# Moving the decay products of a fused SSD + FFN kernel into its prologue, with five halves ahead of pair 1's D

## The chip, the cores and the metric

One core of a Trainium2 chip. The metric is the time of one execution on the device, in microseconds (us). A profile is of one further execution; its span leaves out about 1.7 us of start and end. PE is the matmul engine (PEld its weight loads), DVE is VectorE, ACT ScalarE, POOL GpSimd, SP the queue that issues most loads.

A single execution counts as "slow" here when it lies over 1.5% above the fastest of the same kernel.

## The reference

A chunked state-space layer (4 batches, 8 heads, 768 tokens, head size 32, state size 16), then a gated FFN on its output (3072 tokens, 256 to 1536 to 256). Cut to what matters:

```python
log_a = np.log(np.clip(a, 1e-6, 1.0))          # a in [0.85, 0.95]
for c in range(nc):                            # chunks of 32 tokens
    cum = np.cumsum(la, axis=-1)
    y_intra = (C B^T * exp(cum_i - cum_j) * causal) @ x
    y_inter = (C @ state) * exp(cum)
    state = exp(sum(la)) * state + sum_j B_j x_j * exp(cum_last - cum_j)
out = (np.maximum(y @ w_gate, 0) * (y @ w_val)) @ w_out
```

The kernel works on pairs of 128 tokens. The decay factors are running products of `a`, put into token order by small fp32 products with a picking matrix.

## The kernel before

All engines keep the order of the program. The prologue scales B and C of pair 0, turns them (transposes on PE), forms G = B C^T, masks it, and gets y = (masked G) x + (state) C. That is evicted to `yT`, and the FFN starts: `gvh(b, f, u)` is one "half", four matmuls of 256 columns for feature block f and half-block u of 256 tokens. In the code `adds` is the product of B and x for the state, `inter_wide` that of C and the state, `D_wide` ("D" below) that of the masked G and x, and `decays` ("dec") a small product for the decay of whole chunks. Dummies keep PE busy.

```python
NSHARED = 5                       # five PSUM banks shared; three more: "tp" (turn), "y", "Aps"

def keep_warm(n, rhs=warm):       # warm is a 128x128 bf16 tile of zeros
    w = bank("w", (128, 128))
    for _ in range(n):
        nc.tensor.matmul(out=w, lhsT=warm, rhs=rhs, start=True, stop=True)

def decay():                      # bank "tp"; all batches; fp32
    ...
    for r in range(2):
        for i in range(2):        # 4 products, 64 columns of weights, 8 of output
            nc.tensor.matmul(out=d3[64*i:64*i+64, r], lhsT=cp[:, i*128+r:i*128+128:2],
                             rhs=pick[:, 0, NH:2*NH], ...)
    for k in range(HC):           # 3 products, 128 columns of weights, 64 of output
        nc.tensor.matmul(out=d[:, k]..., lhsT=cp[:, k*128:(k+1)*128], rhs=pick..., ...)

# the order of the program, cut
keep_warm(22); d = factors(); decays(0); keep_warm(8)
...                               # weights' guard and issues, C and B of pair 0 scaled
transp(0, 1, False); keep_warm(4); transp(0, 0, True); tevac(0, A_, V)
scan(0, H); scale_wide(1, 1, P_); scale_wide(1, 0, P_); keep_warm(6)
G_wide(0); keep_warm(7); ...; decays(1); adds(0); ...
inter_wide(0); D_wide(0, ...); turn(1, True); keep_warm(2); yevac_wide(0, A_, V)
load_bc(2, 1, nc.sync); load_bc(2, 0, nc.sync)
...
f0 = gvh(0, 0, 0, True); G_wide(1); decay(); adds(1)
...                               # masks of pair 1, f0()
late = [gvh(0, f, 0, True) for f in (1, 2, 3)]
inter_wide(1); D_wide(1); late[0](); late[1](); yevac_wide(1, A_, V)
late += [gvh(0, f, 0, True) for f in (4, 5)]
for fin in late[2:]: fin()
decay_factors(); ...; halves(0, 1, 0, 1, 2, 3, 4, 5); gv(0, 6)   # u=1, then full blocks
```

## Time and profile before

| | before |
|---|---|
| time, median of 4 fast executions | 124.38 us (124.36 to 124.89) |
| span of the profile | 122.7 us |
| PE busy, share of the span | 118.1 us, 96% |
| first half f0 on PE | 10.53 us |
| G of pair 1 on PE | 11.09 us |
| first half of u=1 on PE | 15.76 us |

Because PE does not wait from 12.77 us to the end, the last row is the one to compare. The prediction shows the lines. Four more of PE, from the timeline of the kernel before (start, length, engine, line, operation; the start-to-start distance of neighbours is the real cost, since the ends are modelled):

```profile
5.79 0.50 PE L189 MATMUL w<-warm 128*128 128x128 bf16 x6
...
10.53 0.38 PE L686 MATMUL gv<-yT,wg 128*128 128x256 bf16 x2
...
11.09 0.42 PE L418 MATMUL g<-CT,BT 32*64 32x256 bf16 x16
...
15.76 0.38 PE L686 MATMUL gv<-yT,wg 128*128 128x256 bf16 x2
```

### The profile page before, as it was taken

The page shows a single profiled execution, that of the slowest core. Times are in us where ns is not written, and L with a number is a line of the kernel's source. Part 1 is how long each engine was busy: PE and PEld are TensorE (multiplying, and loading weights), DVE is VectorE, ACT ScalarE, POOL GpSimd, SP SyncE. Part 2 cuts the span into 40 slices and gives each one's busy share as a digit, 9 for nine tenths or more (in the row PEclk, how much of TensorE's full clock was granted, in tenths as well). Part 3 has the DMA queues.
Part 4 walks back from the last instruction along what each step waited for, and adds up shares of the span by engine and source line. Part 5 has one row for each costly group of instructions (what it writes and reads, how often), then busy time and mean ns, then how long its engine had stood idle before and what let it go on. Part 6 is the DMA issues. An engine that isn't in the chain of part 4 may idle for free.

```text
span 122.7 us, 3665 instructions
## 1 busy us (share of the span) xinstructions
PE 118.1 (96%) x1404; PEld 82.4 (67%) x1404; DVE 88.0 (72%) x200; ACT 76.3 (62%) x169; POOL 48.2 (39%) x108
## 2 busy tenths in 40 slices
PE   6989999999999999999999999999999999999990
PEld 6856784577875478874577864677854678844790
DVE  4798988872799864988763897855987656788410
ACT  0467688835987725786635886545877447876420
POOL 6499989361455127360351806033600033000000
DMA  3999999996979995999999498960580002200022
GB/s 63 220 208 146 171 192 194 189 172 103 115 89 139 143 142 143 103 150 205 150 114 140 154 136 138 110 117 0 189 52 0 0 0 91 85 0 0 0 91 86
DMA packets 77489, 13.93 MB, mean 113 GB/s; under 512 B 70064, under 2 KB 77472, under 8 KB 77472
## 3 DMA queue, kind: packets, MB, share of 16 engines
q1 hardware_dynamic: 70128, 10.61, 54.2%
q0 software_dynamic: 4288, 2.36, 14.1%
q10 hardware_dynamic: 3056, 0.72, 2.7%
q8 instruction: 11, 0.18, 0.6%
q14 instruction: 6, 0.05, 0.1%
HBM read 11.13 MB, written 3.15 MB: 116 GB/s over the span
## 4 chain that ended last, share of the span: by engine, by line
PE 92%; POOL 4%; DVE 1%; issue 1%; DVEq 0%
PE o L713 26%; PE gv L686 21%; PE gate L668 15%; PE val L671 15%; PE y L643 2%; PE g L548 2%; PE w L189 2%; POOL wg L199 2%; POOL bs L322 1%; PE y L632 1%; PE o L707 1%; PE A_ps L601 1%; PE g L418 1%; POOL wv L199 1%; PE y L523 1%; PE dec L262 1%
## 5 line engine op out<-in xcount | busy, mean ns | idle before, releaser
L675 DVE TENSOR_TENSOR h<-r,val 128x512 bf16<-128x512 bf16 x44 | 30.0, 685 | 7.3 <-ACT r L674 7.2
L713 PE MATMUL o<-wo,h 128*128 128x256 bf16 x276 | 33.1, 273 | 0.0
L674 ACT ACTIVATE r<-gate 128x512 bf16<-128x512 f32 x44 | 26.3, 597 | 9.7 <-PE gate L668 9.3
L713 PEld LDWEIGHTS <-h 128*128 128x128 bf16 x276 | 25.9, 98 | 5.3 <-issue 1.7
L668 PE MATMUL gate<-yT,wg 128*128 128x512 bf16 x88 | 26.2, 379 | 0.0
L671 PE MATMUL val<-yT,wv 128*128 128x512 bf16 x88 | 26.2, 379 | 0.0
L692 DVE TENSOR_TENSOR h<-r,gv 128x256 bf16<-128x256 bf16 x56 | 22.5, 419 | 2.6 <-ACT r L689 1.8
L689 ACT ACTIVATE r<-gv 128x256 bf16<-128x256 f32 x56 | 21.2, 386 | 2.3 <-PE gv L686 0.2
L686 PE MATMUL gv<-yT,wg 128*128 128x256 bf16 x112 | 21.5, 273 | 0.0
L686 PE MATMUL gv<-yT,wv 128*128 128x256 bf16 x112 | 21.4, 273 | 0.0
L556 POOL TENSOR_SCALAR_AFFINE_SELECT gs<-gs 128x512 bf16<-128x512 bf16 (+1 forms) x16 | 8.0, 523 | 30.0 <-ACT gs L567 30.0
L573 DVE TENSOR_TENSOR gs<-g,maskUT 128x512 bf16<-128x512 f32 x16 | 10.3, 685 | 11.4 <-issue 5.6
L338 POOL TENSOR_TENSOR tok<-bcr,scaleBC 128x128 bf16<-128x128 f32 x32 | 12.2, 409 | 14.1 <-DMA bcr<-in_B_dram 13.0
L671 PEld LDWEIGHTS <-wv 128*128 128x128 bf16 x88 | 8.6, 98 | 10.4
L668 PEld LDWEIGHTS <-wg 128*128 128x128 bf16 x88 | 8.6, 98 | 8.9
L686 PEld LDWEIGHTS <-wv 128*128 128x128 bf16 x112 | 11.0, 98 | 1.3
L686 PEld LDWEIGHTS <-wg 128*128 128x128 bf16 x112 | 10.2, 98 | 1.9 <-DVE yT L536 0.2
L567 ACT CAST gs<-g 128x512 bf16<-128x512 f32 x8 | 4.7, 589 | 6.7 <-PE g L548 6.7
L656 ACT CAST yT<-y 128x512 bf16<-128x512 f32 x8 | 4.7, 586 | 5.1 <-PE y L643 2.5
L433 DVE TENSOR_TENSOR gs<-g,wmask 128x512 bf16<-128x512 f32 x9 | 5.9, 680 | 2.6 <-PE g L418 2.6
L189 PE MATMUL w<-warm 128*128 128x128 bf16 x49 | 5.5, 284 | 1.1 <-DVE tmask L163 1.1
L189 PEld LDWEIGHTS <-warm 128*128 128x128 bf16 x58 | 5.0, 126 | 1.7 <-DVE tmask L163 1.1
(122 smaller groups left out, 115.8 us busy)
## 6 DMA issues: line engine op xcount, KB each, us to landing
xr<-in_x_dram SPq DMA_DIRECT2D x17, 128.0 KB, 3.2
out_dram<-ob SPq DMA_DIRECT2D x3, 512.0 KB, 3.2
bcr<-in_C_dram SPq DMA_DIRECT2D x17, 64.0 KB, 2.9
bcr<-in_B_dram SPq DMA_DIRECT2D x17, 64.0 KB, 2.9
out_dram<-ob SPq DMA_DIRECT2D x4, 256.0 KB, 3.5
xr<-in_x_dram SPq DMA_DIRECT2D x3, 256.0 KB, 4.1
wo<-in_moe_w_out_dram POOLq DMA_DIRECT2D x2, 384.0 KB, 8.5
wg<-in_moe_w_gate_dram POOLq DMA_DIRECT2D x4, 128.0 KB, 4.0
```

Source lines behind the costliest of these rows:

```text
L189: nc.tensor.matmul(out=w, lhsT=warm, rhs=rhs, start=True, stop=True)
L338: eng.tensor_tensor(out=dst[:, t, j * (1 + t)], in0=src[:, j, :, t], in1=f[:, j, :, 4 * t:4 * t + 4].to_broadcast([128, 2, 4, N]), op=ALU. ...
L556: nc.gpsimd.affine_select(out=dst, in_=dst, pattern=[[0, n], [1, 128]], compare_op=ALU.is_ge, fill=0.0, base=0, channel_multiplier=-1)
L573: nc.vector.tensor_tensor(out=d[:, q], in0=g[q], in1=m, op=ALU.mult)
L668: nc.tensor.matmul(out=g, lhsT=wg[:, k, fs], rhs=yT[:, k, tk], start=(k == 0), stop=(k == 1))
L671: nc.tensor.matmul(out=v, lhsT=wv[:, k, fs], rhs=yT[:, k, tk], start=(k == 0), stop=(k == 1))
L674: nc.scalar.activation(r, g, AF.Relu)
L675: nc.vector.tensor_tensor(out=fst[b][:, f], in0=r, in1=v, op=ALU.mult)
L686: nc.tensor.matmul(out=gv_[:, j], lhsT=w[:, k, fs], rhs=yT[:, k, tk], start=(k == 0), stop=(k == 1), skip_group_check=True)
L689: nc.scalar.activation(r, gv_[:, 0], AF.Relu)
L692: nc.vector.tensor_tensor(out=fst[b][:, f, u * 256:(u + 1) * 256], in0=r, in1=gv_[:, 1], op=ALU.mult)
L713: nc.tensor.matmul(out=o[:, ts % 2], lhsT=fst[b][:, f, ts * 128:(ts + 1) * 128], rhs=wo[:, f], start=(f == 0), stop=(f == NF - 1), skip_gr ...
```

## The change

Its intent: take 1.15 us of fp32 decay products out of the stretch where PE does useful work and put them among the dummies; use the turn bank, free by then, for half f1, so that four halves instead of three stand ahead of pair 1's D; let DVE scale pair 1's B. Its core, with cuts:

```diff
-    a_sb = glob.tile([2 * BH, H], FP32)                 # all batches
+    RL = 2 * (NB - 1) * NH                              # batches 1 to 3: 48 rows for 64
+    nc.scalar.dma_start(out=a_sb, in_=a[1:]...)
...
 def decay(w):
-        # 4 products of 64 weight columns
+        # 2 products of 128 weight columns
         for k in range(HC):
             nc.tensor.matmul(...)
+            if k < HC - 1:
+                nc.tensor.matmul(out=w, lhsT=warm, rhs=warm, start=True, stop=True)
...
-    decays(0)
-    keep_warm(8)
+    nc.vector.memset(wg[0:1, 0, 0:1], 0.0)              # the weights' guard, earlier
+    for f in (0, 2, 4):
+        weights(f, f + 2)
+    decays(0)
+    keep_warm(6)
...
     keep_warm(4)
+    decays(1)                                           # was behind G(0)
     transp(0, 0, True)
...
-    keep_warm(6)
+    keep_warm(4)
     G_wide(0)
     keep_warm(7)
+    adds(0)
     gcopy(0, 0)
     gmask(0, 2, V, True)
-    keep_warm(5, st[0]["gw"][:, 0, 0, 0])               # and 4 more below
+    middle()
+    decay(keep_warm(2))
...
+    tevac(1, None, A_)
+    copy_B(1, V)
     weights(6, 8)
     weights(8, NF)
     weights_out(0, NF // 2)
     weights_out(NF // 2, NF)
     cast_x(1, V)
+    load_bc(2, 1, nc.sync)                              # was ahead of the weights
+    load_bc(2, 0, nc.sync)
...
-    late = [gvh(0, f, 0, True) for f in (1, 2, 3)]
+    late = [gvh(0, 1, 0, True, mm.tile([128, 2, 256], FP32, tag="tp", name="gv1"))]
+    late += [gvh(0, f, 0, True) for f in (2, 3, 4)]
+    late[0]()
     inter_wide(1)
     D_wide(1)
+    late[1]()
+    yevac_wide(1, A_, V)
     late[0]()                                           # these three lines stay:
     late[1]()                                           # work done twice
     yevac_wide(1, A_, V)
```

More of the change, by code (lines that the diff above doesn't have):

```diff
@@ L138 @@
     load_bc(0, 0, nc.sync, nc.scalar)
-    a_sb = glob.tile([2 * BH, H], FP32)
-    nc.sync.dma_start(out=a_sb, in_=a.rearrange("b h (w s) -> (b h w) s", w=2))
+    RL = 2 * (NB - 1) * NH
+    a_sb = glob.tile([RL, H], FP32)
+    nc.scalar.dma_start(out=a_sb, in_=a[1:].rearrange("b h (w s) -> (b h w) s", w=2))
     load_x(0, nc.sync, nc.scalar)
@@ L176 @@
     cp0 = glob.tile([R, 128], FP32)
-    pick = const.tile([2 * BH, 2, BH], FP32)
-    pairs = identf.rearrange("p (h w) -> p w h", w=2)
+    pick = const.tile([RL, 2, RL // 2], FP32)
+    pairs = identf[0:RL, 0:RL].rearrange("p (h w) -> p w h", w=2)
     nc.vector.tensor_copy(pick[:, 1], pairs[:, 1])
@@ L189, in keep_warm @@
             nc.tensor.matmul(out=w, lhsT=warm, rhs=rhs, start=True, stop=True)
+        return w
     wg = glob.tile([128, 2, DF], BF16)
@@ L232, in decays, with scan, decay @@
         nc.scalar.copy(out=dec, in_=d)
-    cp = glob.tile([2 * BH, H], FP32)
-    rmid = const.tile([2 * BH, 1], FP32)
-    def scan(s0, s1):
+    cp = glob.tile([RL, H], FP32)
+    rmid = const.tile([RL, 1], FP32)
+    def scan():
         nc.vector.tensor_tensor_scan(
-            out=cp[:, s0:s1], data0=a_sb[:, s0:s1],
-            data1=zero1.to_broadcast([2 * BH, s1 - s0]),
-            initial=cp[:, s0 - 1:s0] if s0 else 1.0, op0=ALU.mult, op1=ALU.add)
+            out=cp, data0=a_sb, data1=zero1[0:RL].to_broadcast([RL, H]),
+            initial=1.0, op0=ALU.mult, op1=ALU.add)
+        nc.vector.reciprocal(rmid, cp[:, H - 1:H])
     def middle():
-        nc.vector.reciprocal(rmid, cp[:, H - 1:H])
-        nc.vector.tensor_scalar_mul(pick[:, 0], pairs[:, 0], rmid)
+        nc.scalar.mul(pick[:, 0], pairs[:, 0], rmid)
     fac3 = glob.tile([128, 2, 2, NH], FP32)
     scaleBC = glob.tile([128, NB, NC, 2, 8], FP32)
-    def decay():
-        bank_ = mm.tile([128, HC * 2 * NB * 8 + 16], FP32, tag="tp", name="dec")
-        n = HC * 2 * NB * 8
-        d = bank_[:, 0:n].rearrange("p (k w b h) -> p k w b h", k=HC, w=2, b=NB)
-        st["dec3"] = d3 = bank_[:, n:n + 16].rearrange("p (r h) -> p r h", r=2)
-        for r in range(2):
-            for i in range(2):
-                nc.tensor.matmul(
-                    out=d3[64 * i:64 * i + 64, r], lhsT=cp[:, i * 128 + r:i * 128 + 128:2],
-                    rhs=pick[:, 0, NH:2 * NH], start=(r == 0), stop=True,
-                    tile_position=(0, 64 * i), skip_group_check=True)
+    def decay(w):
+        n = HC * 2 * (NB - 1) * NH
+        bank_ = mm.tile([128, n + 2 * NH], FP32, tag="tp", name="dec")
+        d = bank_[:, 0:n].rearrange("p (k w b h) -> p k w b h", k=HC, w=2, b=NB - 1)
+        st["dec3"] = d3 = bank_[:, n:].rearrange("p (r h) -> p r h", r=2)
+        turned = cp[:, 0:256].rearrange("p (i m r) -> p r i m", i=2, r=2)
+        for r in range(2):
+            nc.tensor.matmul(
+                out=d3[:, r], lhsT=turned[:, r], rhs=pick[:, 0, 0:NH], start=(r == 0),
+                stop=True, skip_group_check=True)
         for k in range(HC):
@@ L274, in decay_factors @@
             nc.scalar.copy(
-                out=scaleBC[:, :, cs, 1, :].rearrange("p b k h -> p k b h"), in_=d[:, :, w])
+                out=scaleBC[:, 1:, cs, 1, :].rearrange("p b k h -> p k b h"), in_=d[:, :, w])
     def inverse(b0, b1):
@@ L319, in scale_wide @@
         src = s["bcr"].rearrange("s (t q) j r n -> s j r t q n", t=2)[:, j]
-        f = wfac[:, j, :, :, p]
+        f = fac[:, :, :, 0] if p == 0 and j else wfac[:, j, :, :, p]
         for t in range(2):
@@ L371, in tevac @@
         s = st[p]
-        tp = s.pop("tp")
+        tp = s["tp"]
+        if beng is None:
+            s["CT"] = CT = att.tile([128, 2, 2, 128], BF16, tag="CT", name="CT")
+            for t in range(2):
+                nc.scalar.mul(
+                    CT.rearrange("s t i m -> s t (i m)")[:, t].rearrange(
+                        "s (m r) -> s m r", r=2),
+                    tp[1].rearrange("s r m -> s m r"), tmask[:, t:t + 1])
+            return
         s["BT"] = BT = att.tile([128, 2, 128], BF16, tag="BT", name="BT")
@@ L477, in carry @@
             nc.vector.scalar_tensor_tensor(
-                out=n, in0=T_.pop(c - 1), scalar=dec[:, c - 1:c], in1=st[p]["A"][i],
+                out=n, in0=T_[c - 1], scalar=dec[:, c - 1:c], in1=st[p]["A"][i],
                 op0=ALU.mult, op1=ALU.add)
@@ L675, in gv, with gvh @@
         nc.vector.tensor_tensor(out=fst[b][:, f], in0=r, in1=v, op=ALU.mult)
-    def gvh(b, f, u, later=False):
+    def gvh(b, f, u, later=False, where=None):
         if f == 0 and u == 0:
@@ L682, in gvh @@
         fs = slice(f * 128, (f + 1) * 128)
-        gv_ = bank("gv", (128, 2, 256))
+        gv_ = where or bank("gv", (128, 2, 256))
         for j, w in ((0, wg), (1, wv)):
@@ L768 @@
     keep_warm(22)
-    d = factors()
+    fac = factors()
+    nc.vector.memset(wg[0:1, 0, 0:1], 0.0)
+    for f in (0, 2, 4):
+        weights(f, f + 2)
     decays(0)
-    keep_warm(8)
-    nc.vector.tensor_copy(wfac[:, 1], d)
-    nc.vector.memset(wg[0:1, 0, 0:1], 0.0)
-    weights(0, 2)
-    weights(2, 4)
-    weights(4, 6, (0,))
+    keep_warm(6)
     scale_wide(0, 1, V)
-    nc.vector.reciprocal(wfac[:, 0, :, :, 0], wfac[:, 1, :, :, 0])
+    nc.vector.reciprocal(wfac[:, 0, :, :, 0:2], fac[:, :, :, 0:2])
+    nc.scalar.copy(out=wfac[:, 1], in_=fac)
     scale_wide(0, 0, V)
@@ L781 @@
     keep_warm(4)
+    decays(1)
     transp(0, 0, True)
     tevac(0, A_, V)
-    nc.vector.reciprocal(wfac[:, 0, :, :, 1:3], wfac[:, 1, :, :, 1:3])
-    scan(0, H)
+    scan()
+    cast_x(0, A_)
     scale_wide(1, 1, P_)
-    scale_wide(1, 0, P_)
-    weights(4, 6, (1,))
-    keep_warm(6)
+    keep_warm(4)
     G_wide(0)
     keep_warm(7)
+    adds(0)
     gcopy(0, 0)
     gmask(0, 2, V, True)
-    keep_warm(5, st[0]["gw"][:, 0, 0, 0])
-    cast_x(0, A_)
-    decays(1)
-    adds(0)
+    middle()
+    decay(keep_warm(2))
+    gcopy(0, 1)
+    gmask(0, 0, V)
+    gmask(0, 1, V)
     gmask(0, 3, V, True)
-    keep_warm(4, st[0]["gw"][:, 3, 0, 0])
-    gmask(0, 0, V)
-    gmask(0, 1, V, True)
     pass_on(0, 0)
     carry(0, 0)
-    middle()
+    decay_factors()
+    scale_wide(1, 0, V)
     inter_wide(0)
-    D_wide(0, (2, 3, 0))
-    D_wide(0, (1,))
+    D_wide(0, (2, 0, 1))
+    D_wide(0, (3,))
     turn(1, True)
@@ L810 @@
     yevac_wide(0, A_, V)
-    load_bc(2, 1, nc.sync)
-    load_bc(2, 0, nc.sync)
-    carry(0, 1)
+    tevac(1, None, A_)
+    copy_B(1, V)
     weights(6, 8)
@@ L817 @@
     weights_out(NF // 2, NF)
-    tevac(1, V, A_)
     cast_x(1, V)
-    pass_on(0, 1)
+    load_bc(2, 1, nc.sync)
+    load_bc(2, 0, nc.sync)
+    carry(0, 1)
+    f0 = gvh(0, 0, 0, True)
     def halves(b, u, *fs):
@@ L823, in halves @@
             gvh(b, f, u)
-    f0 = gvh(0, 0, 0, True)
     G_wide(1)
-    decay()
     adds(1)
     gcopy(1, 0)
-    gmask(1, 2, V, True)
-    f0()
-    gcopy(1, 1)
-    gmask(1, 3, V, True)
-    carry(1, 0)
+    gmask(1, 3, V, True)
+    gcopy(1, 1)
+    gmask(1, 0, V)
+    gcopy(1, 2)
+    carry(1, 0)
+    gmask(1, 1, V)
+    pass_on(0, 1)
+    f0()
     pass_on(1, 0)
-    gmask(1, 0, V)
-    gmask(1, 1, V)
-    late = [gvh(0, f, 0, True) for f in (1, 2, 3)]
+    gmask(1, 2, V)
+    late = [gvh(0, 1, 0, True, mm.tile([128, 2, 256], FP32, tag="tp", name="gv1"))]
+    late += [gvh(0, f, 0, True) for f in (2, 3, 4)]
+    late[0]()
+    nc.vector.reciprocal(wfac[:, 0, :, :, 2], wfac[:, 1, :, :, 2])
     inter_wide(1)
     D_wide(1)
+    late[1]()
+    yevac_wide(1, A_, V)
     late[0]()
@@ L843 @@
     yevac_wide(1, A_, V)
-    late += [gvh(0, f, 0, True) for f in (4, 5)]
     for fin in late[2:]:
         fin()
-    decay_factors()
+    halves(0, 0, 5, 6)
     scale_wide(2, 1, P_)
@@ L861 @@
                           wmask.rearrange("p k (m r) -> p k r m", r=2))
-    halves(0, 1, 0, 1, 2, 3, 4, 5)
-    gv(0, 6)
+    halves(0, 1, 0, 1, 2, 3, 4, 5, 6)
     carry(1, 1)
```

## The prediction

> **What bounds the kernel now.** I read the page's busy table first, then the chain of work that ended last, then the first 16 us of the timeline engine by engine, then stretches of busy time.
>
> ```profile
> PE 118.1 (96%) x1404; PEld 82.4 (67%) x1404; DVE 88.0 (72%) x200; ACT 76.3 (62%) x169; POOL 48.2 (39%) x108
> ...
> PE 92%; POOL 4%; DVE 1%; issue 1%; DVEq 0%
> ```
>
> PE (the matmul engine) is busy 96% of the 122.7 us span and is 92% of the chain. The waits view gives PE only 1.5 us of idle time, all before 11 us. After that it never waits, so the time is: when useful matmuls begin to run back to back, plus a fixed amount of work. A change of the first 16 us counts only by what it does to that date. The stretches (columns: length, then busy time of PE, PEld, DVE, ACT, POOL, then clock, DMA share, GB/s):
>
> ```profile
> 8.00:12.77 4.77, 4.50 (x118) 3.16 (x118) 4.26 (x13) 3.28 (x10) 4.75 (x9) 1.00 1.23 162
> 12.77:15.74 2.97, 2.97 (x84) 2.35 (x69) 2.75 (x8) 1.81 (x6) 2.97 (x5) 1.00 1.31 168
> ```
>
> From 12.77 PE is full, but DVE (VectorE) is 2.75 of 2.97 us busy too: it is nearly as tight here. In the chain (start, length), the decay product of all batches sits inside the useful stretch, between pair 1's G and the FFN halves:
>
> ```profile
> 11.13 0.39 PE g L418 x16
> 11.51 0.34 PE dec L257 x8
> 11.85 0.81 PE dec L262 x6
> 12.84 1.42 PE gv L686 x12
> ```
>
> That is 1.15 us of PE which the change wants to hide under the dummy matmuls at 8 us. The durations used below are these rows of DVE and ACT (start, length, line, operation):
>
> ```profile
> 10.19 0.84 ACT L385 ACTIVATE CT<-tp,tmask 128x256 bf16<-128x256 bf16 x2
> 11.55 1.07 ACT L437 CAST gs<-g 128x512 bf16<-128x512 f32 x2
> 11.62 0.69 DVE L433 TENSOR_TENSOR gs<-g,wmask 128x512 bf16<-128x512 f32 x1 [0.40 <-PE g L418]
> 13.16 0.27 DVE L477 SCALAR_TENSOR_TENSOR T<-T,dec,y 128x64 f32<-128x64 f32 x1
> 13.35 0.75 DVE L433 TENSOR_TENSOR gs<-gs,wmask 128x512 bf16<-128x512 bf16 x2
> 14.12 0.75 DVE L692 TENSOR_TENSOR h<-r,gv 128x256 bf16<-128x256 bf16 x2
> 15.07 0.42 DVE L540 CAST yT<-Aps 128x256 bf16<-128x256 f32 x1 [0.20 <-PE Aps L523]
> ```
>
> Consecutive instructions overlap by some 0.07 us, so I count starts to starts: mask from PSUM 0.62, mask from SBUF 0.37, carry 0.20, an h product 0.36, a yT eviction 0.36 on DVE; G copy 0.49, relu of a half 0.32 on ACT; a half (4 matmuls of 256 columns) 0.437 on PE.
>
> **What the Trainium skill says.** "Perfetto Trace Analysis", Identifying the Most-Contended Engine: matmul busy share is no good measure of distance from the roofline. Agreed: the 96% includes 58 dummies, so I go by the chain. "TensorE: Matmul & The Clock Gate", LDWEIGHTS: the load goes by columns, not by contraction rows. The trace agrees: the 48-row and the 64-row fp32 loads of 128 columns both cost 0.135 to 0.145 us a step, 64 columns only 0.04; so going from 64 to 48 rows saves nothing per instruction. Same page, What's actually happening: PE runs at half rate until it has been busy for some 3.4 us. Here 22 dummies take 0.115 us each, and those at 5.8 us take 0.08; fewer dummies might delay that, but PE stays filled. "VectorE: DVE Perf Modes", The perf-mode tier table: a tensor_tensor gains from bf16 in SBUF, not from PSUM. Agrees: 0.69 against 0.41 us.
>
> **Part by part.**
> (a) Front. The weights' guard memset moves ahead of pair 0's scaling, so POOL starts the weight issues at about 3.5 instead of 4.73 us and makes all six in a row. C of pair 0 is scaled straight from PSUM: the 0.21 us copy leaves DVE, but the reciprocal grows from 0.25 to 0.34. The dec product (2 instructions, 0.3 us) now stands before the turn of B on PE, so that turn starts at about 5.7 as before (5.67), and G(0) at 6.45 (was 6.42). On DVE the 0.34 us second reciprocal is gone, so the scan starts at 6.0 (was 6.39) and ends at 6.9.
> (b) Decay in the prologue. ACT does cast x (6.4 to 7.0), G copy (to 7.55), pick (to 7.75). Decay then starts at about 7.8: 2 fp32 matmuls for d3 and 3 for d are 10 instructions (each is two) x 0.135 = 1.35, plus two dummies 0.15: PE is taken until 9.3. Before, pair 0's inter product started at 8.97. So the decay is not wholly free: pair 0's inter and D run 9.3 to 9.87, against 9.83 before, only because D no longer waits for its masks (DVE: the last mask ends at about 9.3).
> (c) Pair 1's B on DVE: 0.49 us at 9.3 to 9.8, in the place where DVE did rmid and pick (0.5 us, moved to earlier and to ACT). B is ready at 9.8 instead of 10.23, but the turn of C now waits for the decay factors' copies to leave the turn bank: ACT 9.45 to 9.87, so 9.94 (was 9.84). yT(0) is done at 10.4 (was 10.38), CT, 0.84 us of ACT after it, at 11.06 (was 11.03). G(1) starts at 11.1 (was 11.09). The earlier B gains nothing, because CT sets G(1).
> (d) Pair 1. PE: G to 11.5, adds to 11.73, f1 at once in the turn bank (free since CT), f2, f3, f4 in G's banks as copy and masks free them (12.25 onwards), until 13.57. DVE: mask 3 at 11.63, mask 0, carry, mask 1, f0, mask 2: 0.62 + 0.37 + 0.20 + 0.37 + 0.36 + 0.37, ends 13.92. D runs 13.95 to 14.3; before it ended at 14.87 with one half fewer done. So up to D the change is ahead by 14.87 + 0.437 - 14.3 = **1.0 us**: roughly the 1.15 us of decay.
> (e) After D. The diff, read literally, runs the product of f2 and the yT eviction, and then the products of f1 and f2 **and the eviction once more**. Nothing removes them, and the first u=1 half reads yT after its last write. DVE after mask 2: f1 waits for its relu on ACT (three G copies, two states, then relu, ends 13.96), runs at 14.02; reciprocal 14.38; f2 14.55; yT 14.9; f1 again 15.25; f2 again 15.62; yT again 15.98 to 16.40. PE can start u=1 at 16.48 (was 15.74). It has f5 and f6 in front, 0.87 us, to 15.17, and then stands idle 1.3 us.
> Sum: 16.48 - 0.437 (one half more done) - 15.74 = **+0.30 us**. Without the repeats u=1 would start at about 15.4, and the same sum gives about -0.75.
> Afterwards DVE has f3 to f6 in hand, 1.5 us late, but a product (0.36 to 0.39) is shorter than a half (0.437) and five banks carry the lag; no further loss. Time: 124.37 + 0.30, and 0.1 for the DMA risk below: **124.75 us**.
>
> **Rivals.**
> 1. Repeats hidden, decay hidden: -0.75 to -1.0 us, 123.5 us. For it: PE is the bound, 1.15 us leave its path. Against: DVE's list from G(1) to u=1 is 4.7 us of work with no slack, and it sets u=1.
> 2. DMA becomes the wait in front. The engines' page shows 220 GB/s from 3 us on; weights starting 1.2 us sooner compete with x(0), which ACT now needs at 6.4 rather than 7.4. x issued at 2.3 to 2.4 with 3.3 us to landing comes at 5.7, but two more 128 KB weights in flight are 256 KB / 220 GB/s = 1.2 us of traffic in the worst case. A late cast moves the G copy, pick and decay: up to +0.5, 125.2 us. Against: the q0 queue's own start is slow (4 us to landing), so most of x is through.
> 3. f2 takes f0's bank rather than one of G's and waits for f0's product at 13.5: PE idles 1.3 us at 12.2, f2 to f4 then end at 14.9, D at 15.2. Since yT then follows D by 0.1, and three DVE steps follow, u=1 starts at 17.0: +0.8, 125.2 us. f1's detour into the turn bank speaks for some bank shortage.
>
> **Range and chances.** The known sum is a gain of 1.0 before D and a loss of 1.3 after it. Either could be off by half a microsecond, and rivals 2 and 3 only add. So 124.0 to 125.5. Two per cent are 2.49 us: more than the whole 1.15 us on offer, so faster by 2% is nearly excluded, and slower by 2% would need rivals 2 and 3 together and more.
>
> **What would show it.** (1) No fp32 decay rows on PE between G(1) and adds(1), but at 7.8 to 9.3. (2) G(1) on PE at 11.1, within 0.3. (3) D of pair 1 ends by about 14.3 with five halves done. (4) Two yT evictions of pair 1 on each of DVE and ACT, and a PE idle of about 1.3 us before the first u=1 half at 16.5, laid to the DVE eviction. (5) From 17 us on the same rows as before, all later by 0.3 us. I am wrong if PE has no idle time before u=1 (then 123.5), if ACT waits for x(0) or PE for a gv bank (then 125.2), or if a later stage moves by another amount than u=1 did.

## The result, and the profile after

The changed kernel takes **128.93 us** (median of 4; three fast executions at 128.01, 128.87 and 128.98, a slow one at 130.19) against 124.38. The ratio is 1.033, 95% interval 1.027 to 1.039. (A ratio is the mean time of one kernel's fast executions over that of the other's in the same rounds, so not quite the ratio of the medians.) The prediction, 124.75 in a range to 125.5, was wrong.

First the page of the changed kernel: span, busy line of PE, chain by engine.

```profile
span 127.2 us, 3657 instructions
...
PE 122.0 (96%) x1395; PEld 84.7 (67%) x1395; DVE 88.2 (69%) x204; ACT 78.2 (62%) x175; POOL 48.0 (38%) x106
...
PE 84%; POOL 6%; DVE 4%; DMA 2%; issue 1%; DVEq 0%
```

PE is busy 3.9 us longer although the program has nine matmuls fewer. So most of the loss is not waiting (PE's idle time grew by 0.6 us, from 4.6 to 5.2): the same work took longer. The PE rows of the changed kernel's timeline say where:

```profile
4.07 0.82 PE L190 MATMUL w<-warm 128*128 128x128 bf16 x6
...
9.00 1.02 PE L259 MATMUL dec<-pick,cp 48*128 48x8 f32 x4
...
11.47 0.66 PE L263 MATMUL dec<-pick,cp 48*128 48x48 f32 x2
...
13.74 0.58 PE L697 MATMUL gv<-yT,wg 128*128 128x256 bf16 x2
14.12 0.63 PE L697 MATMUL gv<-yT,wv 128*128 128x256 bf16 x2
14.68 0.65 PE L429 MATMUL g<-CT,BT 32*64 32x256 bf16 x16
...
16.59 0.38 PE L697 MATMUL gv<-yT,wv 128*128 128x256 bf16 x2
16.80 0.38 PE L697 MATMUL gv<-yT,wg 128*128 128x256 bf16 x2
...
20.12 0.39 PE L697 MATMUL gv<-yT,wg 128*128 128x256 bf16 x2 [0.62 <-DVE yT L551]
```

Read the distances. Two matmuls of 256 columns take 0.38 us at 13.74 and 0.21 us at 16.59. Until about 16.4 us **PE runs at half pace**; the kernel before was at full pace from about 5.6 us. The decay takes 9.00 to 12.06 (the inter product comes next), 3.06 us, where I had counted 1.5. G(1) stands at 14.68, not at 11.1.

The clock column does not show it. Here are two stretches of the changed kernel (columns: stretch, length, busy PE, PEld, DVE, ACT, POOL, then the clock, DMA share, GB/s), all of them at half pace by the distances above:

```profile
12.00:14.00 2.00, 2.00 (x49) 1.34 (x49) 0.76 (x3) 1.28 (x6) 2.00 (x3) 1.00 1.37 183
14.00:16.00 2.00, 2.00 (x39) 0.92 (x38) 1.02 (x4) 1.29 (x4) 0.05 (x1) 1.00 1.15 185
```

The clock reads 1.00. In this view only the distance between PE's rows tells. The reason is in the packed trace, which holds the clock's own records although no view prints them: the first record of the changed kernel begins at 16.39 us, with the full clock, and the view takes whatever lies before the first record as full. Fifteen of the eighteen traces hold such records (those of the kernel before, a_bc_early and a_bf16_fill do not), and they change where the distances change. Every stretch between two changes is a multiple of 3.41 us long.

The loss of 4.5 us of span, split with the prediction's own dates:

| stretch | predicted | measured | off by |
|---|---|---|---|
| start to start of decay | 7.8 | 9.00 | +1.2 |
| decay | 1.5 | 3.06 | +1.56 |
| end of decay to G(1) | 1.8 | 2.62 | +0.82 |
| G(1) to first half of u=1 | 5.38 | 5.44 | +0.06 |
| u=1 to the end, one half more done | 106.50 | 107.08 | +0.58 |
| sum | | | +4.22 |

With the +0.28 that the dates predicted that is the whole 4.5. So there are three things to explain: the 3.58 us up to G(1), of which the half pace is the largest part but not the whole (experiments 2 and 3); the fourth row (which agrees); and 0.58 us behind 20 us.

For the last, POOL's scaling of pair 2 before, and then after:

```profile
15.45 1.53 POOL L322 TENSOR_TENSOR bs<-bcr,wfac 128x128 bf16<-128x128 f32 x4
```

```profile
12.40 1.66 POOL L205 DMA_DIRECT2D wo<-in_moe_w_out_dram  x2
22.30 0.78 POOL L325 TENSOR_TENSOR bs<-bcr,wfac 128x128 bf16<-128x128 f32 x2 [8.24 <-DMA bcr<-in_C_dram]
```

The loads of pair 2's C and B were issued from 14.36 us on (10.44 before), now behind 768 KB of output weights, and loads of this tile took up to 8.5 us to land (at most 5.2 before). POOL waits 8.2 us for it. Everything that POOL does next is late, and at 35 us PE waits 0.4 us for pair 3's turned tile. Whether the one causes the other is the question of the fifth experiment.

### The profile page after: what moved, and what is told of

It reads as the page before. It is cut to its first block, busy times and chain, and to the rows that moved or that the text cites. A ratio compares the mean times of both kernels' runs of the same rounds, so it can differ in the third digit from the quotient of the medians.

```text
span 127.2 us, 3657 instructions
## 1 busy us (share of the span) xinstructions
PE 122.0 (96%) x1395; PEld 84.7 (67%) x1395; DVE 88.2 (69%) x204; ACT 78.2 (62%) x175; POOL 48.0 (38%) x106
## 4 chain that ended last, share of the span: by engine, by line
PE 84%; POOL 6%; DVE 4%; DMA 2%; issue 1%; DVEq 0%
PE o L724 20%; PE gv L697 18%; PE val L682 13%; PE gate L679 13%; PE w L190 4%; DVE h L703 3%; DMA turned<-tok 2%; PE y L654 2%; PE g L559 2%; POOL tok L872 2%; PE dec L263 1%; PE g L429 1%; PE y L643 1%; PE o L718 1%; POOL tok L313 1%
## 5 line engine op out<-in xcount | busy, mean ns | idle before, releaser
L686 DVE TENSOR_TENSOR h<-r,val 128x512 bf16<-128x512 bf16 x43 | 29.3, 684 | 7.2 <-ACT r L685 7.0
L685 ACT ACTIVATE r<-gate 128x512 bf16<-128x512 f32 x43 | 25.7, 597 | 9.5 <-PE gate L679 9.0
L679 PE MATMUL gate<-yT,wg 128*128 128x512 bf16 x86 | 25.6, 379 | 0.0
L703 DVE TENSOR_TENSOR h<-r,gv 128x256 bf16<-128x256 bf16 x60 | 23.8, 417 | 2.2 <-ACT r L700 1.6
L700 ACT ACTIVATE r<-gv 128x256 bf16<-128x256 f32 x58 | 21.9, 387 | 3.6 <-PE gv L697 1.6
L697 PE MATMUL gv<-yT,wg 128*128 128x256 bf16 x116 | 22.8, 278 | 0.6 <-DVE yT L551 0.6
L697 PE MATMUL gv<-yT,wv 128*128 128x256 bf16 x116 | 22.6, 278 | 0.0
L578 ACT CAST gs<-g 128x512 bf16<-128x512 f32 x8 | 4.7, 588 | 6.7 <-PE g L559 6.7
L190 PE MATMUL w<-warm 128*128 128x128 bf16 x47 | 6.4, 311 | 1.1 <-DVE tmask L164 1.1
L444 DVE TENSOR_TENSOR gs<-g,wmask 128x512 bf16<-128x512 f32 x7 | 4.6, 687 | 3.8 <-PE g L429 3.7
L448 ACT CAST gs<-g 128x512 bf16<-128x512 f32 x9 | 4.9, 588 | 2.1 <-PE g L429 2.1
```

The costliest lines, as they stand in the source:

```text
L679: nc.tensor.matmul(out=g, lhsT=wg[:, k, fs], rhs=yT[:, k, tk], start=(k == 0), stop=(k == 1))
L685: nc.scalar.activation(r, g, AF.Relu)
L686: nc.vector.tensor_tensor(out=fst[b][:, f], in0=r, in1=v, op=ALU.mult)
L697: nc.tensor.matmul(out=gv_[:, j], lhsT=w[:, k, fs], rhs=yT[:, k, tk], start=(k == 0), stop=(k == 1), skip_group_check=True)
L700: nc.scalar.activation(r, gv_[:, 0], AF.Relu)
L703: nc.vector.tensor_tensor(out=fst[b][:, f, u * 256:(u + 1) * 256], in0=r, in1=gv_[:, 1], op=ALU.mult)
```

## The experiments

Sixteen kernels ran. The theories, as they changed:

- F: the narrow fp32 products (8 or 48 columns of output) count as idle for PE's clock gate. F1 says that the first move to full pace is lost through dec or the missing dummies; F2 says that the decay takes the pace away.
- D: the number of dummies decides. I: idle PE time decides.
- R: the repeated products and eviction. Q: the order of the DMA issues.

The page "TensorE: Matmul & The Clock Gate" of the Trainium skill (What's actually happening) gives a free-running window of some 3.4 us, by whose activity a gate sets PE's clock to half or full, so executions of one program may differ. They do, as the third experiment shows.

**1. b_dec_early**: the kernel before with one move.

```diff
     keep_warm(4)
+    decays(1)
     transp(0, 0, True)
```

> The kernel before with one move only: the dec product (two small fp32 instructions) goes to where the change has it, ahead of the turn of pair 0's B at 5.5 us; all dummies stay. Theory F (fp32 rows with few columns count as idle for the clock gate, so a warm-up window that holds them fails): PE's steps stay at about 0.11 us for a dummy beyond 5.6 us and the time rises by 0.5 us or more. Theory D (it is the number of dummies): steps fall to 0.08 us at about 5.6 as before and the time stays at 124.4, within 0.2.

Measured: 124.39, 124.45, 125.59 and 126.18 us, ratio 0.999 (0.991 to 1.007). The profiled one, the 126.18, was at full pace from about 4.5 us (it lost its time to a late weight, 0.6, and a late turned tile, 0.9). So dec alone, with all dummies kept, does no harm to the pace in this profile; the 125.59 was not profiled.

**2. a_dec_late**: the changed kernel with dec behind G(0) again and 8 and 6 dummies.

> The changed kernel with the dec product back behind G(0) and the dummy counts ahead of it as before (8 and 6); the decay stays at 9 us. Theory F1 (the first window is lost through dec or the missing dummies, and that alone): PE is warm at about 5.6, decay takes 1.5 us, time 128.9 less about 3.4 to about 125.5. Theory F2 (the decay itself keeps or puts the clock down): PE may be warm at 5.6, but runs at half pace again during or after the decay, and the time stays above 127.

Measured: 128.56, ratio 1.027 (1.022 to 1.033). Full pace came at about 5.4. But then these stretches (columns as above):

```profile
10.00:12.00 2.00, 2.00 (x53) 1.51 (x52) 1.25 (x5) 0.66 (x4) 2.00 (x4) 1.00 1.45 197
12.00:14.00 2.00, 1.78 (x39) 0.75 (x36) 1.03 (x5) 1.25 (x4) 2.00 (x3) 0.55 1.31 163
14.00:16.00 2.00, 2.00 (x27) 1.42 (x21) 1.89 (x6) 2.00 (x6) 0.24 (x1) 0.60 1.17 182
```

Here the column does show it: 0.50 from 12.2 to 15.6 us, which is 3.4 us, right after a stretch with the decay (9.16 to 11.0). All four executions have a mean clock of 0.987 or 0.973; one such fall is 3.4 x 0.5 / 127 = 0.013, so each fell back once or twice. One of the changed kernel's own executions, the 128.01, has a mean clock of 0.973 too. F1 alone is not enough: F2 holds too.

The profile also tells what the decay costs where the pace is full:

```profile
9.16 0.63 PE L259 MATMUL dec<-pick,cp 48*128 48x8 f32 x4 [0.22 <-ACT pick L246]
...
11.00 0.29 PE L509 MATMUL Aps<-CT,Sw 32*32 32x128 bf16 x8
...
13.30 0.65 PE L429 MATMUL g<-CT,BT 32*64 32x256 bf16 x16
```

From 9.16 to 11.00 it takes 1.84 us, not 1.5, and G(1) follows at 13.30, with only 1.1 us of that at half pace.

**3. a_decay_late**: the changed kernel with the decay behind f5 and f6, dec early and few dummies.

```diff
-    decay(keep_warm(2))
+    keep_warm(2)
...
     halves(0, 0, 5, 6)
+    decay(None)                                         # without its two dummies
+    decay_factors()
```

> The changed kernel with the decay products out of the prologue, after the halves f5 and f6 (so 1.2 us of PE at full pace come back there); dec stays early and the dummies few. Theory F2 (decay keeps the clock down): PE is warm by 9 us and the time falls to about 125.5 (-1.5 of decay at half pace, -2 from the rows after it at full pace). Theory F1: PE is still at half pace until some 12 us or later and the time falls only by about 1.5 to 2, to 127.

Measured: 127.42, ratio 1.018 (1.011 to 1.024). PE rows of its profile (in brackets a wait and what ended it):

```profile
4.08 0.67 PE L190 MATMUL w<-warm 128*128 128x128 bf16 x6
...
10.70 0.38 PE L695 MATMUL gv<-yT,wg 128*128 128x256 bf16 x2 [0.18 <-DVE yT L549]
10.91 0.38 PE L695 MATMUL gv<-yT,wv 128*128 128x256 bf16 x2
11.26 0.42 PE L427 MATMUL g<-CT,BT 32*64 32x256 bf16 x16
```

Full pace from about 4.4 us on, and G(1) at 11.26. That is near my 11.1, but my 11.1 had the decay ahead of it, and here it is gone; with it, a_dec_late stood at 13.30. So the decay was not hidden among the dummies even at full pace. Here, at 15.73 to 16.97, it takes 1.24 us, about what it took in the kernel before, and throws nothing back in this profile (one of the other three executions, the 128.29, has a mean clock of 0.987, one fall). Of the 2.7 us of span above the kernel before, 0.8 is there when u=1 starts (one half more counted off), and behind it PE waits 1.3 us for pair 2's and pair 3's tiles.

Set its first row beside that of the changed kernel: the same PE program up to there, 0.67 against 0.82 us for the same six dummies. One execution came to full pace at 4.4 us, the other did not. So it is in part luck, as the page says of the free-running window.

**4. a_norepeat**: the changed kernel without the second `late[1]()`, `yevac_wide` and `late[0]()`.

> The changed kernel without the second products of f1 and f2 and the second eviction of yT(1). My prediction's step (e) gave these 1.05 us of VectorE ahead of the first u=1 half. The trace shows PE idle 0.62 us there, as f5 and f6 cover part: theory R expects 128.9 less 0.6, 128.3, with the clock as slow as before until 16 us.

Measured: 127.97, 0.96 less than the changed kernel, ratio to before 1.021. PE was at half pace until about 17.4, later than in the changed kernel's profile. First DVE's rows of the changed kernel with the repeats, then those without:

```profile
18.65 0.42 DVE L551 CAST yT<-Aps 128x256 bf16<-128x256 f32 x1
18.99 0.74 DVE L703 TENSOR_TENSOR h<-r,gv 128x256 bf16<-128x256 bf16 x2
19.65 0.42 DVE L551 CAST yT<-Aps 128x256 bf16<-128x256 f32 x1
```

```profile
19.26 0.42 DVE L551 CAST yT<-Aps 128x256 bf16<-128x256 f32 x1 [0.48 <-PE Aps L534]
19.61 1.41 DVE L703 TENSOR_TENSOR h<-r,gv 128x256 bf16<-128x256 bf16 x4
```

Without them the first half of u=1 follows f6 without a wait, at 19.95. The repeats cost about what R expects: the wait of 0.62 us, or 0.8 if one counts from the end of f6 (19.34) to u=1 (20.12) in the changed kernel.

**5. a_bc_early**: the loads of pair 2 issued behind pair 1's scaling.

```diff
     scale_wide(1, 0, V)
+    load_bc(2, 1, nc.sync)
+    load_bc(2, 0, nc.sync)
```

> The changed kernel with the loads of pair 2's B and C issued behind pair 1's scaling on VectorE, at about 10.3 us as in the kernel before, and no longer at 14.4 behind the issues of the output weights. Theory Q (C of pair 2 stands behind 768 KB of output weights in the DMA rings, so POOL scales pair 2 only at 22.3, and pair 3's turned tile is late for its G): POOL scales pair 2 by about 18, the wait of PE for the turned tile (0.4 us) goes, and the time falls by 0.4 to 0.6. Rival: the shift of 0.5 us behind 24 us has another cause, and the time stays within 0.2.

Measured: 125.46, 128.30, 128.44 and 129.13. The profile is of the 128.30; it came to full pace at 16.2, as the changed kernel's did, so the two can be set side by side: span 126.6 for 127.2, POOL's scaling of C at 15.44 for 22.30, and no wait for the turned tile. Between these two profiles that is 0.6 us, as Q expects. But Q is not shown. Four other profiles with the loads issued as late, at 14.5 to 16.8 us (4, 6, 7 and 9), have no such wait and take 106.5 to 106.8 us from u=1 to the end; b_dec_early and a_dense, with the loads at 10.4 and 8.3, wait 0.9 and 0.7 us. Nor do the times part: apart from the 125.46, 128.30 to 129.13 here, 128.01 to 130.19 in the changed kernel. The 125.46 is the best sight of the rest: I read the 3.0 us below the median of the others as an execution that came to full pace early, but it was not profiled.

**6 and 7. a_fp32_fill and a_bf16_fill**: four dummies behind each decay product; the second also with `cp` and `pick` in bf16 (its result passed the comparison).

> The changed kernel with four bf16 dummies behind each of the five decay products in place of two in all. Theory F (the fp32 rows with 8 or 48 columns leave the array so idle that their window counts as idle): with 20 dummies in it the window counts as busy, PE steps are 0.11 us for two matmuls of 128 columns (full pace) from 12 us on, and the time falls by 1 us or more in spite of 1.1 us more of dummies at 9 us. Rival P (any work on that place delays pair 0, and the pace is a matter of luck): time rises by about 1.

> As the run with fill, but the decay's operands in bf16 (result may be less exact on purpose): five single products in place of ten fp32 instructions, among the same 20 dummies. Theory F: full pace from at most 9 us on and through 12 to 16 us in every execution, time below the fp32 run with fill by about 1 us. Rival (the clock falls for idle PE time in these microseconds, not for fp32 rows): the pace at 12 to 16 us is half as in the changed kernel, and the time stays near it.

Measured: 131.11 (one execution at 128.46, the other three slow) and 129.22. Both profiles were at half pace from the start, until about 20.2 and 17.1. So my expectation for the bf16 one was a miss: with dec early and dummies missing PE missed its first move, and 20 dummies with bf16 decay between 9.3 and 12.7 did not bring it back. Theory F as first told, fp32 rows as the only cause, falls.

**8. b_fp32_dummies**: the kernel before, nine dummies at 7.5 and 8.5 us replaced by five fp32 products.

> The kernel before with one suspect alone: the nine bf16 dummies at 7.5 and 8.5 us are replaced by five fp32 products of 128 columns by 48 (ten instructions) that nobody reads. Theory F: the window that holds them fails, PE runs at half pace for about 3.4 us somewhere between 9 and 16 us, and the time rises by 1.5 to 2.5. Rival P: PE waits for the same masks there either way, and the time stays within 0.5 of before.

Measured: 125.15, ratio 0.999; no fall in the profile, and one execution of four with a mean clock of 0.986, one fall. Ten fp32 instructions there are harmless nearly always. F2 needs more than their number.

**9. a_warm_bf16**: dec late, dummies 8 and 6, and the bf16 decay with four dummies behind each product.

> Both suspects removed from the changed kernel at once: dec back behind G(0) with the dummy counts of before (8 and 6), as in the run with dec late, which was warm at 5.4 but at half pace again from 12 to 15.5; and the decay in bf16 with four dummies behind each product. Theory W (a window of about 3.4 us must hold mostly full-width bf16 products; first dec and the missing dummies spoil the first window, then the fp32 decay spoils the one at 9 to 12): warm at about 5 and no half pace after that, recorded clock 1.0 in most executions, time 126.5 or less, which is 2 below the run with dec late. Rival (the decay throttles by its place, not by its fp32 rows): half pace at 12 to 15.5 again, 128 or more.

Measured: 129.23; the rival was right. Full pace at about 5.5, half pace from 9.0 to 15.7, twice 3.4 us. Before that fall PE had stood idle 0.6 us at 5.7 (for B, whose DMA was late) and more around 8.3 and 9.1. The other three executions have a mean clock of 1.00 and were not profiled; whether they were at half pace from the start or slow for another reason is open.

**10. a_best**: dec late, dummies 8 and 6, bf16 decay with two dummies, no repeats, early loads.

> A try for a version that beats both: dec late and dummies as before, decay in bf16 at its new place with the two dummies of the change, no repeated products and eviction, loads of pair 2 early. By theory W: full pace throughout, no 0.6 us wait before u=1, no late turned tile: 123.6 to 124.2, that is 0.3 to 0.8 below before on an equal chip. If the window at 9 to 12 still fails (fewer dummies than the run with fill), 126.

Measured: 128.20, all four within 128.03 to 128.25. The bf16 decay took only 0.7 us, and PE still fell to half pace, from 11.0 to 14.4: PE was busy 0.69, 0.78 and 0.83 of the three microseconds from 8 to 11. No fp32 decay is left here, and a_dense (14), with the same bf16 decay and the waits filled, keeps the pace: idle time is a cause of its own. (The loads of pair 2 went out at 11.36 here, just ahead of the output weights, and C was still late, at 19.9.)

**11. b_bf16_decay**: the kernel before with the decay in bf16.

> The kernel before with the decay's two operands in bf16 and nothing else: 7 products instead of 14 fp32 instructions, 0.3 to 0.4 us of PE instead of 1.15, in the same place. PE is the bound there, so I expect 0.7 us less than before; if VectorE or ScalarE set the pace of the stretch (it is 2.75 of 2.97 us busy), 0.3 or less.

Measured: 124.09, 124.14, 124.19 and 124.93, ratio 0.997 (0.991 to 1.003). The products take 0.35 us where fp32 took 1.15, but D then waits for its masks, so 0.3 us is gained at best, and the interval holds no gain for certain.

**12 and 13. b_front and b_fewer**: the kernel before with 6 and 4 dummies for 8 and 6; b_front with dec early too.

> The kernel before with the front of the change alone: dec at 5.5 us and 6 and 4 dummies for 8 and 6. Theory W: in some of the executions (those whose window edge falls near 6 to 7 us; a third to a half) PE misses its first warm-up and stays at half pace until 9 us or later, so times scatter: some at 124.4 to 125, some 0.5 to 2 above. If all stay within the scatter of before (124.4 to 126), the front alone is not enough and it takes the decay behind it.

> The kernel before with 6 and 4 dummies for 8 and 6, dec where it was. Dec early with all dummies gave no late start in 4 executions; both together gave 5 of 6 executions at 126.0 to 126.6. If the dummies do it: most executions at 126 again. If it takes both (the window needs some 25 dummies of about 30 and either alone leaves enough): at most one in six above 125.5.

Measured: b_front 124.54 once and 126.00 to 126.58 five times (the two of 126.58 slow); b_fewer 124.87, 125.20, 126.21, 126.47, 129.47 and 129.49 (the last two slow). Over the fast executions alone both ratios are 1.007 (to 1.014 and 1.012 at most), the same within 2%: it is the pace that tells. PE rows of b_fewer's profile, the 126.47:

```profile
4.08 0.82 PE L189 MATMUL w<-warm 128*128 128x128 bf16 x6
...
11.74 0.59 PE L686 MATMUL gv<-yT,wg 128*128 128x256 bf16 x2
12.12 0.63 PE L686 MATMUL gv<-yT,wv 128*128 128x256 bf16 x2
```

Half pace at 12 us, with nothing changed but four dummies. So it is **the four missing dummies** that make PE miss its first move to full pace, in most executions and not in all; dec is not needed for it. The 129.5 were not profiled and stay unexplained.

**14 and 15. a_dense and a_dense_fp32**: no repeats, dec late, early loads, and dummies in every wait of PE up to pair 1's turn; bf16 and fp32 decay.

> The changed kernel with dec late, bf16 decay, no repeats, pair 2's loads at 8 us, and dummies in every wait of PE up to pair 1's turn (8, 8, 9, 3, 8, then 2 behind each decay product, 6, 6). Theory I (idle PE time and narrow products in a window of 3.4 us make it fall back): no fall back, gv halves at 0.22 us for two matmuls from the first on, u=1 at about 15.5, time 124 to 125. Rival (the place of the decay, or the zeros in the dummies): half pace at 11 to 15 us again in most executions, 127 or more.

> The same with the change's own fp32 decay. If fp32 rows weigh as idle: falls back in most executions although every wait is filled, 127 or more. If only idle time counts: stays at full pace, and takes 0.9 us more of PE at 9 us than the bf16 one, 125 to 126.

Measured: a_dense 126.03, 126.62, 126.68 (and a slow 130.24, not profiled); a_dense_fp32 128.00, 128.45, 129.60 (and a slow 131.06). The first half f0 on PE, first in a_dense, then in a_dense_fp32:

```profile
12.71 0.38 PE L699 MATMUL gv<-yT,wg 128*128 128x256 bf16 x2
12.93 0.38 PE L699 MATMUL gv<-yT,wv 128*128 128x256 bf16 x2
```

```profile
14.83 0.63 PE L699 MATMUL gv<-yT,wg 128*128 128x256 bf16 x2
15.26 0.54 PE L699 MATMUL gv<-yT,wv 128*128 128x256 bf16 x2
```

0.22 us a pair against 0.43. With every wait filled and the decay in bf16 the pace holds; with the fp32 decay it falls back, in all four executions (mean clock 0.987, 0.971, 0.986, 0.971). So both idle PE time (a_best) and the narrow fp32 products (a_dense_fp32) can take the pace away. But a_dense wins nothing (ratio 1.012, 1.005 to 1.018): pair 0's inter product comes behind the decay and its dummies, at 11.36 instead of 8.97, and f0 is at 12.71 instead of 10.53. So with dummies enough to hold the pace the move still loses.

**16. b_best**: bf16 decay in the kernel before, and one more half ahead of D.

> The kernel before with bf16 decay and one more half (f4) ahead of pair 1's D, then f5 and f6 behind it and 7 halves for u=1. In the run with bf16 decay alone PE waited some 0.35 us for the masks of D; this fills it. Expected 0.5 to 0.7 below before; 0.3 or less if VectorE, which then has one more half's products, sets u=1.

Measured: 125.57 (124.92 to 125.97), ratio 1.005, a miss: PE waited 0.9 us at 15.8 for the `w_val` columns of f6, which the earlier half now reads before they land. No version here beats the kernel before for certain.

**What a window needs.** I laid stretches of 3.41 us, the step of the clock records, back from the moment when the pace doubled (where a trace has no records, from PE's rows), and counted the dummies in them. Of the first stretches, those of seven profiles that ended in full pace hold 25 to 27 dummies (before, 1, 2, 3, 8, 9, 11); those of five that did not hold 14 to 19 (the changed kernel, 4, 6, 7, 12), and that of a_best, with 24, did not either. The missing dummies make at most four of the difference. The rest is where a stretch lies: the seven begin at 0.9 to 2.2 us, the five at 2.7 to 3.8, when more of the first 22 dummies are over. So a_decay_late, with few dummies, still holds 26. No profile with all the dummies has stretches that lie like those of the five; that all the dummies would carry these too rests on the times. Of the 40 executions of the kernel before, one took 126.16 and one 296.88 us (unexplained), all others at most 125.99; of the twelve of b_front and b_fewer, nine took 126.00 or more. Nor is the count an exact rule: in a_best a stretch with 20 dummies and G(0) was enough, and in a_warm_bf16 one with 21 dummies and bf16 decay, later, was not. What exactly is counted stays open.

## Why the prediction was wrong

- **Step (b), and step (a) under it, failed.** The prediction put the decay at 10 x 0.135 + 0.15 = 1.5 us, "PE is taken until 9.3", and took all PE durations from rows at full pace. The decay took 3.06 us from 9.00. That is the mis-sized term: PE ran at half pace until 16.4. At full pace it would have been 1.84 (a_dec_late). The doubt ("fewer dummies might delay that, but PE stays filled") was waved away with the wrong measure: the busy rows stayed filled, but not with dummies. b_fewer shows that four dummies fewer do it, a_dec_late and a_dense_fp32 that the decay does it again where the first move succeeded.
- **Not all of it is the pace.** Step (b) also took the decay to hide among dummies at almost no cost to pair 0. At full pace `pick` was ready at 8.10 (a_decay_late; predicted 7.75), the decay took 1.84 us, and 2.3 more led to G(1) (a_dec_late). Added up, an estimate of mine, G(1) would have stood at about 12 instead of 11.1, so about 1 us of the 3.58 belongs to this and about 2.5 to the pace. Rival 2 showed a little: in the changed kernel DVE waited 0.5 us for pair 0's B, and not ACT for x.
- **Step (c)** held in its order: C was ready on ACT at 14.29, B on DVE at 13.95. But G(1) came behind f0 at half pace and waited for neither.
- **Steps (d) and (e)** held in sum: G(1) to u=1 in 5.44 us against 5.38. DVE's list set it, as predicted: the second eviction started 4.97 us after G(1), against 4.88. PE came later (half pace until 16.4), so its wait for that eviction was 0.62, not 1.3 us. The repeats were predicted from the diff and are shown by a_norepeat.
- **"All later by the same amount"** failed by 0.58 us, 0.42 of it PE's wait for pair 3's turned tile. I had looked for DMA trouble at x of pair 0 and not at pair 2, where the order of two issues turned around. That this order is the cause is not shown (experiment 5).
- **Rival 3** (f2 waits for f0's bank) did not occur: f1 to f4 ran back to back.
- **The chances** were wrong because the greatest thing on offer was taken to be the 1.15 us of decay. The pace of PE was the larger stake: 3.0 us by my reading of the 125.46, 1.5 to 2 us in b_front.

## What to carry to other kernels

Dummies in a prologue are no filler: before you trade them for small products or drop a few, ask what the pace of PE will be after it, and measure several executions, since a marginal prologue succeeds in some and fails in others. Read PE's pace from the distance of equal matmuls, not from busy shares or from the clock column. When one queue's issues move earlier, look for the loads of another queue that now come behind them, and see in several profiles whether the engine that sets the time ever waits for them.

## What the Trainium skill lacked or had wrong

- "TensorE: Matmul & The Clock Gate", What's actually happening: it names a window of about 3.4 us and "sustained" activity, and this agrees with the recorded fall of 12.2 to 15.6 us. It gives no measure of how busy a window must be, and nothing on how narrow or fp32 products count. Here first stretches with 25 to 27 zero dummies moved to full pace and such with 14 to 19, and one with 24, did not, although PE was busy 91 to 100% of them; idle time and narrow fp32 products each took the pace away again.
- Same page, Part 1, Seeing it yourself: it warns that the records of the gate can't be fully trusted. Here 3 of 18 traces hold no clock record at all; in the other 15 the records change where PE's distances do. The 1.00 at 12 to 16 us of the changed kernel is no wrong record: the view fills the time before the first one, at 16.39 us.
- Same page, What's actually happening: it puts the ramp's penalty below 1% of a typical kernel span. Here a late ramp cost more, with small prologue products on the path: by my estimate about 2.5 us of 124, 2%, in the changed kernel.
- "DMA: Bandwidth & Descriptors", Issuing engines are not separate DMA queues: agreed. It gives no size for a small load behind a large one: the 128 KB loads of pair 2's C and B behind 768 KB of weights took up to 8.5 us to land, against at most 5.2 before.
